# The first pair's queries and keys go ahead of the first weight block, and the planner's port rule is rewritten

## The chip, the cores and the metric

The kernel runs on one core of a Trainium2 chip. The metric is device time in microseconds of one execution; lower is better. Each time is the median of several runs.

## The reference

Two parts follow each other: attention with a threshold, and a gated MLP over its output. All arrays are float32 as seen by the caller; the batch is 8, with 8 heads of width 64 and 576 positions.

```python
scores = scale * q @ k.T                      # per batch and head, 576 x 576
thresh = max(scores, axis=-1) - tau           # tau = 0.02
scores = where(scores >= thresh, scores, -1e9)
attn = exp(scores - max); attn = attn / (sum(attn) + 1e-9)
x = attn @ v                                  # heads side by side: (8, 576, 512)
h = gelu_tanh(x @ w_in)                       # 512 -> 1024
u, v = halves of h
v_n = layer_norm(v) * g_ln
v_s = w_sg @ v_n + b_sg                       # over positions, 576 x 576
out = x + (u * v_s) @ w_out                   # 512 -> 512
```

The weights `w_in` and `w_out` reach the chip as 64-bit words; the kernel splits each into a high and a low float32 part itself.

## The kernel before

The work is written as 5368 *steps*, each a few instructions on one engine. Attention goes over 32 pairs of heads (4 pairs in each of 8 batch entries); a pair has nine score tiles of 128 rows. For a tile, TensorE forms scores (L807 for the first four pairs, L832 later), VectorE takes row maxima (L841), GpSimd subtracts the threshold (L847), ScalarE takes exponentials (L867), VectorE selects and sums (L874), TensorE transposes (L539), ScalarE copies the transposes out of PSUM (L982), and TensorE multiplies with the values (L1008). The MLP's products (L1105) of one batch entry are mixed in among the attention of the next.

The order in which steps are issued is fixed by a table, `PLACES` (L35): a compressed list with one position for each step. `order` (L319 on) sorts the steps by it; every engine then works through its own steps in that order, one after the other. The list holds steps of all engines, so moving a step in it changes something only if it passes another step of its own engine.

All loads are issued by SyncE (SP), in order, onto one queue. The first steps of each engine matter here:

- SP loads, in this order: weight block `w2` (L578; the block is 128 rows by 512 columns of `w_in`, 512 KB), the first pair's queries (L727, tile `rq`, 288.5 KB: they carry `tau` as an added column), its keys (L727, tile `rk`, 320 KB), the queries of a later pair, weight block `w0`, and so on.
- VectorE derives from `tau` the scale of the queries and the offset of the threshold (L555 to L557). Later it does three bit operations on the weight block (L596, L602, L604), then the first row maxima (L841).
- GpSimd converts the low words of the weight block in place (`w_bot`, L586), then scales the first queries (`q_scale`, L757), then clamps the weight block (`w_clamp`, L591), which VectorE's bit operations need.
- ScalarE takes absolute values of the block's upper words (`w_abs`, L582).
- TensorE does three short warm-up products (L545), the first scores (L807), then the products that give the low part of the weight block (L613).

While it is built, the kernel reckons with a clock of its own (`Planner.run`), from durations written into it. That reckoning does not set the order, which is the table's, but it chooses the PSUM banks: there are eight, and a tile of scores, transposes or products takes the bank (or the two) that the reckoning has free first (`place_in_banks`). In the reckoning, a VectorE operation flagged as using two SBUF ports and a GpSimd operation are not let run together. The flag is set in `_record` (L281 and L289): `ports > 1`, where `ports` counts the SBUF operands that are read, with one more for a `tensor_scalar` that reads SBUF.

Of the kernel before, what the change touches and what calls it, by code (L numbers as in the profile page):

```python
# [32 lines left out]


PLACES = (  # L35
    "c-qxi3v^Xgdd|1c>)w0r`;nU`c@q*KKnS4;s4&7PYqUN_eDtA?+Nzzk`cS)8+p(iEGuoLh3+S}EbjtF9k4~pJjujO}&~ZR!aOj9ZK^X%G0^t>d"
    "JjCSm`}es(kR&7lSM7y+&)NH&{Xf3{`~Us#<av4iKYl#@)wlB7Yc{X<?6K(+mL0wHexc{Ybv?Z#<;n2at#^F7*KA%tFZA_p_X!J*YV}SO)9<kF"
    "WqEzv^dozK;juffACWz$kUdzt`<CtD3}cel+wL59ynYe;g7<wr@8^lWcK43IH?WRAb$SEqIPOPYZ?^aOruPMz{RVnq9bR5uAA^3z1M4^uk`w$G"
    "0{+9+aS~^St78DH`qPoux6Z-%(L3jk>F@@xBX0;;<(<lp-WTswI=qweV<4<fl^=O07uP;>FsH*COg!?2ndkla(N{hUKF__O^XfF}Ro)Qe;hlaC"
    "eknS7Q_&m9V{fQ2?>8RDH;|#!_Po=J`Kj#o`ppk-==tHD*k1Lc(;GCe`ZBOz0YlEgywl{B*N4Yni5&C>s2!)J<BJ}9eN^nzsfmNhId6D-)NteB"  # L40
    "on~!6^D+0%u#Ub?0(<)2@B00m>iJ2{M*o|sH`H}Q9`$7zdiw1ezI4aWj62>?9Y6V;^MC8OH(>jAN=3u<-~0bS^)u?YH$2C_Y{$JplY7XH=W^Wp"
    "s!;vQi1^^websW@8+08TJX40{xHp_M@dkz3a9QmQ-ML<q@qN>mKmTXSQ)#4kr!P|TT6Sfk2pc_Thg+P_9Dt89u&3@T%pg$FJ`1;8c-4RWofRzY"
    "x)Fh@9-|?a+?zx?JR{z@HWB_bjCfOha__k&^7kgqom24&@SO>Gx&<GNcxc~u!m8rFId?PxhyeTNc~dN-3eiH`exuW4L;)A*xOn3PJ~zxHzL)Z<"
    "ldw5^Lvu^`(^iCmvma_l$+j98D5(3ZKmEhDF?ALYt-SjYu0gPT6IW(b?Q*CrD)wM^5D2B??*M_Q>#FrOVi=D%C@~Aic_V@l#$t0CTTM79!FzD6"
    "0vy4AJ4m6d7-$b6>mcl?>rq-f3$&$Ct>CL8u_3)93?q^?-=~Hee1=a9nqPzuU|Lxm#BagZCgQD8*snlo*rmL*LeTn|jWkL!Xnlp=j6f6xixIi&"
    "dqC1jV;$nQ8R~Mof-s$tpxtf>f_OVbB}wdng(Naq5#~)r@ZDN;C;}13F8!;p)WJ-Fw({8uI!G^r(^8#Fe@|q>;v6EQ)GlnJFej#V09KKuaKNB~"
    "Fn02{3<*39N}7g_B5;{uG?=TPj0$vPK>~$>F;Xt_QA}-j$HtjG#^<WzoUv`*)8|v4S)<kgrdi0Rv^^Rhi#NF<TZT>M;Q%Z%jqPIA6pET3Ae!gn"
    "#cQyL(Xnf>mN=>L1m|VK0u&{<;-)ndM)H1N{gib^4<4USn^hsUl9mq9Q#<+0tit*t2&e^kO@R3${6fsU0lTpbMo(lWUT(o^zHK+-4eAKR5x~bN"
    "=R4`dZ0b%w5h2NMDtze*PW^){wi3jHq7r<Q4uyD=Vj={Kh(jB!&qL?n1!9_*j;&Z_bHOaU&?;{lfia>AcAU}Q&Sjvl(`oJx?v+HUsqV-x-loD8"
    "9K;9;FK&QXb-+H7h+wnm2%uVhC=aILMJ|t3l8<YZQaBe&N8)2TU=^dCs`y?fDUlTWDh}HUyT6^Hj)u}U$*;@b;tw;bQz8~m?8g6)D#2#7(HP=u"  # L50
    "t8GHia<^SB<H?{`NKSkM&rik%1v@wjYk0vZ>?2m<M`fVL!1$$e#E*jdg*S8R*}M3YudtmEBoumL6vi8O7a10zq1ed>al`K9*e)S<8-f&B3>J*{"
    "Y&doXTltnzO2)k{DN;#yRrB=gT3e~({QUN_l^4C|UzpaR6di@KO0b8ZF>{j)42e`u_qIwgnTbUXrzT<}Hj`K8MR>Lm8zhorB@>~l@d-tg@OGqW"
    "*(kf?(u;Y2R>Oyt<kiCu&?)k1znC9UpHmBYrT-(5PbzfM%<ybHLmcc%$umhi>X?c(tXNhh){Bk_WZWiH@OHH7cBbPmW?skpu?;WIqK-v#gp?&X"
    "#21;uM}#e~Qv{cvCTcWjLnN+kV1`BUbLvcv!8@&3C6O$!b}OP%#=Ks|MCG&MgM@X-eXhi#`MdL|<H>tuKBytF(u7*#Vb{<svV;T{GlRI02?pCr"
    "k~UOop&A>r_$3{*%JIHpDJTvb<Uj$}hO&E7?(I`<E~Jh*A9dC9GWTK5XIw3sJU%E1t!!7q2W}J=-jzB$2EUQ?N|Haz1;=Lmx&^<ZRc1y!R%Q)K"
    "u~hq!sMt?_egD$g6h6CjYaRX2IcS&Rec{>&F5fQsGB&tW=oX<1AMqw0XGk@d51@_EglkhPn{~{Cfz(E-at(_5oG1`(+AtH}z545v*HU}?0$zS{"
    "w}4cF523kvNQW?1An|dE1FYww!@L|%QeJd2ZCGXz8W!{htjO_7(c4CT-z24hS_!OL@)X<y?zqSke@^8;epKu%HMUAkmU^`@hXpmECi`1-n+RFa"
    "$TrE;GUmsY7{!HfAR(lcdb}yd1@4H?$ZJN+%_I+@b@q%a%jm#$=8qmRyK&b-%8fZvuZ*PB)=h%x3@N_|W$1sKSbIGlls)w-bm29{m(IgW<E6kO"
    "G!82T#jzyGP89flFiA>LD{QNM^x8?Qam(v6SE;cglUyN`jJHYYiSzbjad4LNs;IWzxIhyQ*5Ta}$jVe&Clra;#W#tAO}x~f;JIrhzGtTw-pcE`"
    "3;2qYH9wTP8|1fx2&g1>nXp++vuI<*;6_Ul#f)0!&#zbk+|g(oi7m3S1RJH|R7ZMPOY(U)5e6q#e6xW%CRcA8&3HVxKn#qB)^V$rlBTgKZN?gM"  # L60
    "BpPKMq;lK66pLw3qK@^#kP?`+ww6dKPPkd?15U(Ki34<9VvaICx_0_wb<{Eaz~Pa+{PVrE*Db(CHaOub(up9UK=MU-sbX@qi{n5->KXEjNX?bB"
    "(rv-YR`Sa1b_&sMP-!i3Uco($xF$`$vHH4iQ25C7Cl$Qh_FohhC^Ln!Mw&7<a_mfI5-ZQD*I-jb3)TuSY-F%du{ch1mRzj48%v^HNRWXv9FiR6"
    "&Ouxdz5nVa3Xj&kehH@*%=I_GL(shi^tQ&BcSy|Z)owD2H&@{)hAHBhhop1_@yB?g06SFK-sC8(bd+aHMefvC71##F{O;Qb9Sk*9Zkfn<JTy->"
    "pIS?jHffOmd;Q|KS;ADu@dtz|I8F9i2NiLH4zaB(NBd-k2o6iw4pEwAyx-Qfy_P1c%PzZ7xO+wFwx@Wx_b~yZNK-Z;I+%lYewE}40!bXEvi#lY"
    "DorB0ka_r?LdYR^$BT}TienGcI#x*DZqPWC>qhgz*7+1ZHGji6@#A5MM=8x^2`?~r5j2in2EsnVGUiAv31G60N7P{Fx}5nDZo=wTsg8)1<2{3U"
    "E){yG?tR9PC+B0%U6LQ?R4%@TI+_oO-U2DNLD}=A&Supl^(M(tKt59$Nn0em3K|*8dX*b}q!1sE!8($b&7|~KsN)8+g;kkbk#oqj5)WT;4RzF3"
    "uWzD`pWQ)JBL;f7G~nQH_488X&&5i%ZWzs4zghNT=@kiGkXUvzaoiX>Gs1Gism0qYXpDx-+9Ek<mhKvnx@zX-qm@_JlK-vesN;wK%4xTTwVf1A"
    "P{#TMV!?Xdr$lTS3kQlcR^;b3Qh);_(AF#PI48`QL{ecK6XTaU<~6!0eSX3N!9(Zm7;(`rB<AyE>JQW^!R4%qE#~X~CcB#b5WYrRk5C1-pm#-5"
    "Iq`Y`dVhcMLVw4cgkQ;m39MF>bcI&%Sp+lS?>7QoRNoiU)BE*ZFfG3^T3jP-jQ^OqmBrtRV@YmDqC*Zi#X?<_i*3O$gLz9#P7Z7#Egn|zq+;xB"
    "oP{tGGu|#3fHfmvv7W3m<=DipK~AB&UR1=d)S3c6k%k}m8((o_SYJZ^s8a*QiYT8S-L0zwinNWH`4u5iJI!C<@0D&!Iv->^^h~;2$MWX2)ndB="  # L70
    "-_a7>CXFx8M)I5BI)Nt^NEZ2hj?Ml^I!|9}ifyonE`sAvB#Fg8lJj4KQGjB>W|<Tk8$a-$Kd#S$)PoqW%Vhz|C+ZCfPsp?hX@yv8KafWbrk2Vh"
    "Iez%|=}(P+WckRq`ZCmilO>|UfA(wrLbTk{qnw?&xM}y%aGqfQ>P>&GM-lxyno8$t({#r}M@{CGeM~?pUA$8ogV<3+s$o%TJfSymjTrtdXv=wJ"
    "qAz5zKB#d-VwA~9MCI$%b^j@&8<;FnslCr=Wx7goBBwE^4NGRw%gR)dKWNj{%APN;UCGK96W<e-VUqV<{5l3QCwS}+tSQiEnyUrA5`Qj@D*Tgy"
    "W1o6DR_gCBRlZjt+#_;a|9M#Rv5^z@QD|MvRY>qWSC-I7FO#@AJg-q~B=e|%F+$e?g!5krY3a>ACtnU3etSvl)4Ib+N|`H_KMmw;3M6y%6;Ces"
    "sWy9j6HhjT@3}IO#N!6FhSW2ST$NC{Q2XJ}|DnD#pXEn2*6UH6j?VS7J_m%uZb_=J58Wh^|5lxA5l1Sl{Ar=g(G3MpEcz7}3s}RLX3b&62!$4k"
    "k&U>(7x)?!dDi%jR#^L-w3#St(T^rSCi)%ha3fL&KJ}Ayyk&@qIg?gt;#YV1hl2IoW;E5S6c2N6>DT3N0`gfQ0S*y^s5<7&oe$~?<9=O7aor+)"
    "uJZA%WCZRMC~^poq9K#~Nap)cr}$jDG@ptwa??s4Cm|<dc!b!pt_dG2T`U$ZIQUE0Q9k=IlGag}3mfm3-3{jy>B5MAXS5@JJ{qzs>RmSr*F^Ma"
    "2}wr{-x{rM6XXvCm?5BEB4r@XlWE-VgisjNnS$P_K1%<7>(-lfuKZN*sXix0QsNz%<5eU}P?~g(`i@o6@!KWffl$B~SP0W$0yu#nRF3_RW^{I!"
    "M@490i6)u4-WRw?MC%6Bpvd2dUN!xQPcCWDCI$SX&Ba&(|Ic6kx@G?5r9_T+y1MP7egg4x%@^#^{FROgEWr7>DC-3`+~@CEm-ussG#m|oU*iKK"
    "zLt`R_vZ37mScj?V7)8r{;&6FihoglE=Bd`nRA~(3SxDBuH@;h9zpw!;$v*mX`#W|Yv%S+9IL8et&)9RtwmuNmRjS7Vmn-kz&1bGe=kixee<KV"  # L80
# [1312 lines left out]
```

## Time and profile before

| | us |
|---|---|
| median of 3 runs | 970.79 (970.67 to 971.47) |
| profiled execution | 967.75 |
| its span, first to last instruction | 966.0 |
| TensorE busy | 946.5 (98%) |
| VectorE busy | 662.7 (69%) |
| ScalarE busy | 664.3 (69%) |
| GpSimd busy | 562.8 (58%) |

The busy times are of the one profiled execution and add over the whole span; the engines work side by side. The mean granted TensorE clock of that execution was 0.996 of full speed. A line such as L757 is a line of the kernel's file; tiles go by their names without buffer numbers, so `rq` is a tile of raw queries, `rk` of raw keys, `w` a raw weight block, `room` its working copy, `nm` a tile's row maxima, and `all_banks` is PSUM.

### The profile page before, as it was taken

Reading aid. Unit: us, or ns where it says so; the run is one execution under the profiler, and the core shown is the slowest. Engines: PE = TensorE matmul, PEld = TensorE weight load, DVE = VectorE, ACT = ScalarE, POOL = GpSimd, SP = SyncE. Lnnn points to the kernel's source line nnn. Section 1 sums busy time; section 2 is a strip of 40 time slices with the busy share of each in tenths; the row PEclk is TensorE's granted clock in tenths of the full one; section 3 lists DMA queues with packets and bytes.
Section 4 is the critical chain, followed back from the end, with each engine's and each line's share of the span. In section 5 each row is a group of like instructions: output and inputs, shape, how many; then the busy total and the mean of one; then the engine's idle time right before and its main releaser. Section 6 shows DMA issues by size and latency. Waiting matters only on the chain.

```text
span 966.0 us, 19828 instructions
## 1 busy us (share of the span) xinstructions
PE 946.5 (98%) x6822; PEld 811.0 (84%) x6822; DVE 662.7 (69%) x1409; ACT 664.3 (69%) x1395; POOL 562.8 (58%) x997
## 2 busy tenths in 40 slices
...
GB/s 291 138 121 111 20 112 71 124 128 137 113 97 107 123 127 91 86 114 124 91 108 98 135 124 92 90 110 139 117 80 102 99 142 122 93 65 38 14 13 50
DMA packets 60236, 100.39 MB, mean 104 GB/s; under 512 B 15220, under 2 KB 23655, under 8 KB 60136
## 3 DMA queue, kind: packets, MB, share of 16 engines
...
## 4 chain that ended last, share of the span: by engine, by line
PE 83%; DVE 6%; ACT 5%; POOL 3%; issue 2%; DMA 2%; SPq 0%; POOLq 0%; ACTq 0%; DVEq 0%
PE all_banks L1105 38%; PE all_banks L1008 15%; PE all_banks L832 14%; PE all_banks L539 13%; DVE nm L841 1%; ACT p L867 1%; PE all_banks L807 1%; DVE p L874 1%; DMA qz<-qhi 1%; PE all_banks L613 1%; ACT pt L982 1%; POOL ot L1308 1%; DVE vv L1088 1%; PE all_banks L991 1%; DMA rq<-in_qT 1%
## 5 line engine op out<-in xcount | busy, mean ns | idle before, releaser
L841 DVE TENSOR_REDUCE nm<-all_banks 128x1 f32<-128x576 f32 x288 | 209.9, 752 | 59.4 <-PE all_banks L832 52.4
L867 ACT ACTIVATE p<-all_banks,nm 128x576 f32<-128x576 f32 x256 | 185.0, 740 | 88.0 <-DVE nm L841 86.4
L874 DVE SCALAR_TENSOR_TENSOR p<-all_banks,nm,p 128x576 f32<-128x576 f32 x256 | 204.0, 814 | 56.0 <-ACT p L867 28.3
L982 ACT ACTIVATE pt<-all_banks 128x512 f32<-128x512 f32 (+1 forms) x320 | 164.6, 554 | 23.1 <-PE all_banks L539 22.5
L539 PE MATMUL all_banks<-ident_r,p 128*128 128x128 f32 x1152 | 172.0, 275 | 2.8 <-ACT pt L982 1.4
L832 PE MATMUL all_banks<-ks,qst 128*128 128x288 f32 x560 | 157.2, 314 | 0.3
L539 PEld LDWEIGHTS all_banks<-ident_r,p 128*128 128x128 f32 x1152 | 135.9, 141 | 21.0 <-issue 4.1
L1008 PE MATMUL all_banks<-pt,rv 128*64 128x320 f32 (+1 forms) x1024 | 138.1, 411 | 0.1
L847 POOL TENSOR_TENSOR nm<-columns,nm 128x1 f32<-128x1 f32 x288 | 53.9, 192 | 143.7 <-DVE nm L841 132.2
L832 PE MATMUL all_banks<-kl,qz 128*128 128x288 f32 x448 | 123.6, 295 | 0.0
L1105 PE MATMUL all_banks<-wsh,z 128*128 128x288 f32 (+2 forms) x512 | 113.1, 299 | 1.4 <-ACT z L1206 0.9
L832 PEld LDWEIGHTS all_banks<-ks,qst 128*128 128x128 f32 x560 | 102.4, 189 | 11.9 <-issue 6.3
L1008 PEld LDWEIGHTS all_banks<-pt,rv 128*64 128x64 f32 x1024 | 69.6, 136 | 49.2 <-issue 7.0
L1105 PEld LDWEIGHTS all_banks<-wsh,z 128*128 128x128 f32 x512 | 85.0, 188 | 2.4 <-ACT z L1206 1.1
L832 PEld LDWEIGHTS all_banks<-kl,qz 128*128 128x128 f32 x448 | 84.7, 189 | 0.3
L1105 PE MATMUL all_banks<-xh,wih 128*128 128x288 f32 (+2 forms) x256 | 78.3, 306 | 0.0
L1105 PE MATMUL all_banks<-gh,woh 128*128 128x288 f32 (+2 forms) x256 | 76.2, 301 | 0.0
L1105 PE MATMUL all_banks<-gh,wol 128*128 128x288 f32 (+2 forms) x256 | 76.2, 299 | 0.0
L1105 PE MATMUL all_banks<-xh,wil 128*128 128x288 f32 (+2 forms) x256 | 76.2, 298 | 0.0
L1105 PE MATMUL all_banks<-xl,wih 128*128 128x288 f32 (+2 forms) x256 | 76.0, 297 | 0.0
L1105 PE MATMUL all_banks<-wsl,z 128*128 128x288 f32 (+2 forms) x256 | 75.3, 296 | 0.0
L1105 PE MATMUL all_banks<-gl,woh 128*128 128x288 f32 (+2 forms) x256 | 75.2, 295 | 0.0
...
## 6 DMA issues: line engine op xcount, KB each, us to landing
...
```

What stands on the lines that cost most here:

```text
L539: nc.tensor.transpose(out, x, ident_r.bitcast(F32))
L613: nc.tensor.matmul(t["acc"], a, x, start=(j == 0), stop=(j == 2))
L807: nc.tensor.matmul(st["s", h, i][:, a, 0:HALF], st["q"][rows, qo:qo + P], st["k"][rows, lo:lo + HALF], start=True, stop=True)
L832: nc.tensor.matmul(sc[:, a, 0:HALF], w, x, start=(j == 0), stop=(j == len(terms) - 1))
L841: nc.vector.tensor_reduce(nmax, st["s", h, i][:, :, 0:HALF], AX.XY, ALU.max, negate=True)
L847: nc.gpsimd.tensor_tensor(thr, toff, st["nm", h, i], ALU.subtract)
L867: nc.scalar.activation(target(h, i), st["s", h, i][:, :, 0:HALF], AF.Exp, bias=st["nm", h, i])
L874: nc.vector.scalar_tensor_tensor(dst, st["s", h, i][:, :, 0:HALF], st["thr", h, i], dst, ALU.is_ge, ALU.mult, accum_out=st["l"][:, c:c + 1])
L982: nc.scalar.activation(dst, src, AF.Copy)
L991: nc.tensor.matmul(tp[:, 0:D], pm[:, MAIN:KW], both, start=True, stop=True)
L1008: nc.tensor.matmul(acc[h * D:(h + 1) * D, 0:w], st["v"][:, o:o + D], unit(h, a)[:, kt, 0:w] if kt < NM else tail_unit(a)[:, 0:w], start=(k ...
L1105: nc.tensor.matmul(st["acc"], *term(j), start=(j == 0), stop=(j == n - 1))
```

## The change

Two edits. The first replaces the table of positions. Read out, the lists agree in everything but their first 18 entries, and there in the place of five steps: the loads of the first pair's queries and keys, the first step on `tau`, and two of the warm-up products.

```
place   before                      after
0       warm-up product             load queries, first pair
1       warm-up product             load keys, first pair
2       load weights w2             load weights w2
3       w_bot w2        (GpSimd)    tau 1           (VectorE)
4       load queries, first pair    w_bot w2        (GpSimd)
5       tau 1           (VectorE)   tau 2           (VectorE)
6       tau 2           (VectorE)   tau 3           (VectorE)
7       tau 3           (VectorE)   warm-up product
8       q_scale         (GpSimd)    q_scale         (GpSimd)
9       w_abs w2        (ScalarE)   warm-up product
10      w_clamp w2      (GpSimd)    w_abs w2        (ScalarE)
11      w_word w2       (VectorE)   w_clamp w2      (GpSimd)
12      w_word w2       (VectorE)   w_word w2       (VectorE)
13      w_hi w2         (ScalarE)   w_word w2       (VectorE)
14      w_word w2       (VectorE)   w_hi w2         (ScalarE)
15      w_mul w2        (GpSimd)    w_word w2       (VectorE)
16      warm-up product             w_mul w2        (GpSimd)
17      load keys, first pair       warm-up product
18      first scores    (TensorE)   first scores    (TensorE)
```

Taken engine by engine, only SP's order differs: before it loads `w2`, queries, keys; after it loads queries, keys, `w2`. The orders on TensorE, VectorE, ScalarE and GpSimd are the same in both lists.

The second edit is the flag: a VectorE operation now counts as using two ports only if it is a `tensor_scalar` with all its operands in SBUF and more than 64 elements in each of 128 rows. It emits no instruction; it enters the reckoning that chooses PSUM banks.

```diff
 PLACES = (
-    "c-qxi3v^Xgdd|1c>)w0r`;nU`c@q*KKnS4;s4&7PYqUN_eDtA?+Nzzk`cS)8+p(iEGuoLh3+S}EbjtF9k4~pJjujO}&~ZR!aOj9ZK^X%G0^t>d"
+    "c-qxi3zSvWdA{F1uY2#g@5kJEGVd8?cnz<iGoV6*C@WeY5g$#eMs3w*tv=MQ)iyRNX|zd}1vITLwXCT4XqsS*6%|F)7?1=*BMu5m96%5lo`O8Y"
...
         first = writes[0] if writes else reads[0]
-        ports = sum(not a.psum for a in reads) + (op == "tensor_scalar" and not reads[0].psum)
+        ports = 2 * (op == "tensor_scalar" and not any(a.psum for a in (*reads, *writes)) and reads[0].size > 64 * P)
         rows = first.shape[0]
```

More of the change, by code (lines that the diff above doesn't have):

```diff
@@ L35 @@
 PLACES = (
-    "c-qxi3v^Xgdd|1c>)w0r`;nU`c@q*KKnS4;s4&7PYqUN_eDtA?+Nzzk`cS)8+p(iEGuoLh3+S}EbjtF9k4~pJjujO}&~ZR!aOj9ZK^X%G0^t>d"
[L37 to L80, printed above, removed]
@@ L81 @@
-    "|7iWy+O{8+(z~iF-=k0TR{g(Fl?OT"
+    "c-qxi3zSvWdA{F1uY2#g@5kJEGVd8?cnz<iGoV6*C@WeY5g$#eMs3w*tv=MQ)iyRNX|zd}1vITLwXCT4XqsS*6%|F)7?1=*BMu5m96%5lo`O8Y"
+    "nbYsz=Q0d3Gt3OQVlUi#&fe$j|MC6b|L=cKzzg{Q`0?~t-^y=~*+9?P?&;%}9li8?q3if{T|FcPWY~S{9h>ek8|dSO-rnsD^f10#t9QJZK8L+8"
+    "3-of+hwOfa-FIFeBD+o^d!TmrF5AOt#w5_w?mTzAJ`wwz_q{#u<B7g@_Kd&Rzm8sYdj0D-=0~6>+k1V}`<%=^1Kqz4FA(Tu(8suc9mhj*oF9Y0"
+    "f5<vc;LK2U^n+DjIs(1x9Ecx1bFN#5H*g(+L0}a)nIAnb-pO=$C*((eSe-0C0w)&NUUM+7!y8CE0z=I6zWnGd9|oT1-r#w43iT>5$ar|Co`YYA"
@@ new lines @@
+    "j-FKX`t#TuY|Q(N$FU7$Ftt5!YB4{V-Cm#h;SD}NyyM%eK6H8m=2dS7_9<Y{IT$!aUU|KE{H4f2ub<j+N;*F8vDZt*K9!m{keu^|wnq&$9^NU|"
+    "_R}A8?=<V^?If_P_x-NV&&i&j&}{U*nR<g=H|SAsmZ7W9uHg%J{Peiv4c74!&pCfw$Gv{rx05Ows{h{q2dbY|$GxFB_C-7H4Vc`6c08Zs-j{{y"
+    "Uqr+QzV6GG<KBSl*ua@GB*(p>q=`2m)P~AxZ}86bm`omMedFhUp*)pAW@qLCHMeC)Hin4Nb!Ma`_^AWvNA{FGMOg$Z+h^jY^RM`?f3QMj`>sc@"
+    "y2}_HPwh@26PcdayE+;9B!a|*#?<b!O%&`-ncJt}CEz<_@nj1=9QMGT??hDPJ+p6{03ZtNpX*JwjB3P+aO?F>mk|S8pyR^zWBJ@LQ}|xmt4YD;"
+    ">~+m8kxyC?0nU7&9i>}pVW6<#Z~pvG+eS86K&<M{hYSUExM>4dW>x(wP&riY!p;y7&LrLjf-%=sYi-2Qgx4uC2gi9miZDiDV+NZ|I4H%taIHcd"
@@ new lines @@
+    "!T&f&qr3!Y4<qLw;;3s;Rx%T`Wt>{ZSL?7Yvn>K6nls;{hFW}zj}4k%jQ3$$IUL0Az}Lp(&EeRuKxx>ayo^G~`k9RkO0#HviQWuD426pjz2kd8"
+    "%E@3261ExM=k5!^bm~C6-BN_`R+vgs*aizJWU(y5o668T_2^IpB7q(HS7C{R83Jw9)0K3PUWTTo_b&MZ;f#oLhz?gfu!X{$xY`C-#g@VWg9;+p"
+    "&fjt*@gyi|Dmse6Wri`@TmfZNq7(CzD1v;_E(%aWZFk1Um|ezas^hFtZQhgTQlD9?)&Qni#HX}9mKcRMxFT1M4d&q>EHi_xV%B7eninLR=i>RR"
+    "u#nNQ>#>?RsV0K+B4GiFlU#Abs<Cyv-_tmGjnRci=h0?Wgw3R-L-f>kJ~OMawip6xAzl?={tUkqGq1x=EQQe(oq-oyu##`v&3K(U!U+WN5i0mj"
+    "COM0`Gmk|{@*9d?xQtW(B#W&i@t~+A-=srf-lUlbp<?3D2J5r%S$K|^CZ}ODR@huH6VJ8En?`V?sDhnf^tW;u=<76^`~ABmk!ou?3QD%9NF@hx"
@@ new lines @@
+    "g2Ia%Bvu`;k0hhmC^~|uQ6I>Isd%2t<5lG2YNZs;#*#XGL<g)Av{Mz|+e=EM#J<YIw!+SDr>SFfS)1h7rEl_w8MRj;mPqcz|B@=9X0*{5;%lod"
+    "LeL7gT`o;z&`TsIzJ_NfVV!~<8je-GU^w;=EAgW$*kzz;$!zhXuyMhSoO=2W{uC%|B?L)@t~iD9#@#`NMQJFu^FhL}_i}8P61#OFiYx&O#=ABg"
+    "JB!VH%P1q`-jWolqPwbj+BL1M)NyV>`<cp%-SuxkD4eFFP*y2+5j19Qih&`KD(K#3DJC<p(Bag0tj9+3%DezikHb2N<S5BRs2Y4s5v9DXGc6nC"
+    "w_SW8@6Q<hK^1xR;C*z8eA+MON7ZN4LSE_rNEVO^due857M>ywc9rCrq#bok!75fPs|ssH$5=9M11fntLUlUR@K-ag;r*!5&(EZeg|mf}r8vYF"
+    "nZieeEwIxBm!ApLXwZgeLfgO$i{Tg4nHq_=Td_hSS!nH4M5Ua0y@H9#XC(&->*9M{iAVEy=TgVxcgcK6Lt?RL3r%3x(k!xs1Qs(xIG+gy+e(o("
@@ new lines @@
+    "RBE9H>vQ-O9keR&o?<B|i5TQSA=id;yVCBhlW#1dj@cjXYvg6lgPhO0S~PilP!d|%u7nRNOL6b;CNvVimGnxHKd%Um&G=0Veow2+taz-<T9jdl"
+    "_9I!jpZxlli)T^ztg_7w^h4*MU5@vJYs0vFtK`e5&=R3rlrDV8n?!;k)m%P+HbN7rPcLuQF%JdP>#52$DC#q!K)7kc41D*>uTox1{jKwPdFW07"
+    "sT3bTbMuf6VZ2b{<CFwh&qarMDITZ1*d*Gp)FL!2=%cYL&nrc5$MO3HDGk(1VAbL$;2v<tL?8Q0D*y4rVrQALS!%M>tMz#-s0p>X-=Wh)*osBB"
+    "NT!xEKQ_fFE{p?7A+6No4RJ1ThkZ(3Gg@vobqKAqre9u82d*)H_!F}ecPyaXxFhw-NJ(woAec^<@{4em{<n#>*W!NJQ?I~2ysG%pIe4K-3OvGN"
+    "uv}0aMUresq3;Kiqzv`Kw)%&!p12Y>y(V*28Y?o%6++2)i<F)OZ$A<TXF4y7YTHc+G?7pP-YJEwOlNdLk%;^FCULNdm-;52xmx0TW@f?7yskNq"
@@ new lines @@
+    "uQ)mL1F5?qemjVON@0fyo7FUjHdYL7v?Nj7sAvBCniaqufwnqql9i=cFBPXI+QnK@z`OBaM}TEtA59&TYPO7EJno+_1}4I5xK&F@)7X?XV--0P"
+    "i?I$;x$RzzMYJc`z<Oaw3CvlWOQjSi-JJD4Clcx80lF?RM>!u|J?)VO>X>%ma2+o{x|{a8g;>u9CsIv15hN5!z9=tULay%PIGB`rhJs>Jb2+Va"
+    "Td=&9yfQnTBD5P+T2GvpaZe+zDU)xkyyj~ZUYGf}l9yY4PGP}vQz&a>C}Tax&Lk$W@~lP;Hbt~xwE)9L1`8C6<5Xwyg_^tZ6xxLZSxCbn$x-1P"
+    "#CfrMube>Pv4+<!;?(>({swpmy0?Jd))?~+iFu>iNoMip3OvCuMIG~yl#UR-fyWB5O_lFX4aagvdA3yKy&9`R+n|`=e;eV0;R#in#xoud%$3cj"
+    "-jbwE8RY+NzxZvGFg0-eKA{RtmA%$MWx}9CZ0jn}K8YcM!xFYll;#-kw{&f<r^)J)ORg90UY5S)3104gM8GK4lue2b=Ad0rE%}0A3WuqzU}vUU"
@@ new lines @@
+    "lgKV&9=@v(cF5f((GgY&>|$ESi^$t`8VBhc5W2s09)(XSST{!ecu?X|Msr!h3(Xw_jboRAu#d2eIZ{i4n55$oGuXMl!u*I#z{*ysj)+&_U4wZp"
+    "6?(hweMXWe=VJC9k{@SPExL+2nh%NILMgW)+4H5&=F~*>2FX!KK2sS<TP(Z^8ClADnHzny2p^5a8j_aHr1V#4;0CjaRhe6nbI7!k4_<T?b=23a"
+    "oj@HwyN#$u4Rmp7(81xFXQjxWjpc0JFoLyyqwK}fD-ya8vFv2xxN+>w3d;?r9&fRrF&Zvwi{zkLwqscOiW!%VP+mhz!MC2FjvxFxr`=lCc2YD+"
+    "8Ecb>hZ=RC618P494OXUk)Kyd0S=Ntn=iwooG{}ONrf>?j9=-P*XpM9*|GP94xO`Y*ag3on9r4|KT#_Lmoq9inXmbq>`L}S_zG=3LKWPC-VsR^"
+    "#Oprj{r&m#{T*{6ek}{evRYBnWm>_fQA~%w-w1dyeP2XR@6~sqjQqxFajmp5{$u7=4u3C>rMMl54mseI2z5~*wuK@L=1p-qIk1Jacv!*Xim|hC"
```

12 lines of the change are left out of this document (added).

## The prediction

> **What bounds the kernel now.** I read the page's totals first, then the chain of waits at the start, then the queues that feed that chain. The totals, from the page:
>
> ```profile
> span 966.0 us, 19828 instructions
> ...
> PE 946.5 (98%) x6822; PEld 811.0 (84%) x6822; DVE 662.7 (69%) x1409; ACT 664.3 (69%) x1395; POOL 562.8 (58%) x997
> ```
>
> TensorE (PE) is busy for 946.5 of 966.0 us, in a fixed order. So once its stream runs, whatever delays the start of the stream delays the end by as much, and only its 19.5 us of idle time could give anything back. The change is at the start. The chain of waits there, in order of time (start us, us, what):
>
> ```profile
> 1.18 4.89 DMA rq<-in_qT
> ...
> 6.09 0.15 DVE columns L555
> 6.24 0.07 DVE columns L556
> ...
> 6.34 0.82 POOL rq L757
> ...
> 7.24 0.62 POOL room L591
> ...
> 7.89 0.71 DVE all_banks L596
> ...
> 8.62 0.70 DVE room L602
> ...
> 9.41 0.43 DVE w L604
> 9.84 0.68 DVE nm L841
> ```
>
> The first queries land at 6.07 us (1.18 + 4.89), the scale is derived from them (L555, L556), GpSimd (POOL) scales them (L757). But the chain does not go on to the first scores. It goes through the first weight block: its clamp on POOL (L591), its three bit operations on VectorE (DVE, L596, L602, L604), and only then the first row maxima (L841), which stand behind those in DVE's queue. Each step starts within 0.1 us of the end of the one before it, so this stretch has no slack to give.
>
> **The change, part by part.** It is a matter of queues. SyncE (SP) issues the transfers; POOL takes its work in order. Both timelines (start us, us, engine, line, operation, count, and in brackets the idle time before), and what SP waited for in the first 12 us:
>
> ```profile
> 0.73 0.39 SPq L578 DMA_DIRECT2D w<-in_w_in  x1
> 1.18 0.42 SPq L727 DMA_DIRECT2D rq<-in_qT  x1
> 1.64 0.43 SPq L727 DMA_DIRECT2D rk<-in_kT  x1
> ...
> 5.31 0.40 SPq L727 DMA_DIRECT2D rk<-in_kT  x1
> 6.08 0.33 SPq L660 DMA_DIRECT2D w<-in_w_sgT  x1
> 7.19 0.33 SPq L578 DMA_DIRECT2D w<-in_w_in  x1
> 7.92 0.33 SPq L727 DMA_DIRECT2D rk<-in_kT  x1
> ```
> ```profile
> SPq L578 <- DMA rk<-in_kT: 0.8, 1, 0.8
> ...
> SPq L660 <- DMA rq<-in_qT: 0.4, 1, 0.4
> ...
> SPq L727 <- DMA w<-in_w_in: 0.3, 1, 0.3
> ```
> ```profile
> 5.37 0.65 POOL L586 TENSOR_SCALAR w<-w 128x512 f32<-128x512 uint32 x1 [4.07 <-DMA w<-in_w_in]
> 6.34 0.82 POOL L757 TENSOR_SCALAR rq<-rq,columns 128x576 f32<-128x576 f32 x1 [0.32 <-DVE columns L556]
> 7.24 0.61 POOL L591 TENSOR_SCALAR room<-room 128x512 f32<-128x512 f32 x1
> ...
> 11.54 0.74 POOL L757 TENSOR_SCALAR rq<-rq,columns 128x576 f32<-128x576 f32 x1
> 12.36 0.66 POOL L586 TENSOR_SCALAR w<-w 128x512 f32<-128x512 uint32 x1
> ```
>
> From its ninth transfer on SP issues each one when an early one lands, so its restarts are landing times: the weights at 5.31 (the ninth waits for the first), the queries at 6.08, the keys at 7.19, a later pair's queries, fourth in the queue, at 7.92.
>
> (1) *The moved transfers.* The queries are now issued at 0.73, the keys at 1.18, the weights at 1.64. The three together are the same bytes as before, so the last of them, now the weights, should land when the last of them did before, the keys at 7.19: 1.88 us later than the weights' 5.31. The bounds: with nothing ahead slowing it, the weights need the 4.58 us of before (5.31 - 0.73) from their new issue, and land at 6.22; if the fourth transfer's packets mix with theirs, they land with it, at 7.92. I take 7.19, because the four landings come one after the other, which says queue and not parallel service. The queries land at 5.31 or sooner (first place, fewer bytes than the weights that landed then), the keys by 6.08 at the latest, the second place's landing of before. The transfers behind these three keep issue and landing within the bound just given.
>
> (2) *What the early queries release: nothing.* DVE derives the scale at once, so the 0.32 us that POOL idled ahead of L757 goes. But the order of POOL's queue is untouched: L586, which reads the raw weights, stands ahead of L757. The wait for the weights, 4.07 us at 5.37, grows, and the scaling of queries that have long been there is stuck behind it; then L591 behind that. From the weights' landing: 0.06 to POOL's start (5.31 to 5.37), L586 0.65, a gap of 0.08 (11.54 + 0.74 to 12.36), L757 0.74 (the undisturbed later row; the 0.82 ran beside a DVE operation that now runs earlier), a gap of 0.08. L591 starts 1.61 us after the landing: at 8.80 instead of 7.24, **1.56 us later**. By the bounds: 7.83 (0.59 later) and 9.53 (2.29 later).
>
> (3) *TensorE and ScalarE at the start.* The first scores follow L757's end, 8.72, instead of 7.16. They must be done when DVE gets to the first maxima, at 9.84 + 1.56 = 11.40. Rows for the warm-up products, for these scores and for later sets, and the granted clock in stretches of 2 us (the column PEclk, 1.00 is full):
>
> ```profile
> 1.61 2.93 PE L545 MATMUL all_banks<-pm 128*128 128x256 f32 x6 [1.61 <-DVE pm L520]
> 7.31 1.24 PE L807 MATMUL all_banks<-rk,rq 64*128 64x288 f32 x8 [2.77 <-DMA rk<-in_kT]
> ...
> 12.28 2.29 PE L807 MATMUL all_banks<-rk,rq 64*128 64x288 f32 x8
> ...
> 17.50 1.33 PE L807 MATMUL all_banks<-rk,rq 64*128 64x288 f32 x8 [0.98 <-ACT tt L997]
> ```
> ```profile
> 6.00:8.00 2.00, 0.69 (x6) 0.68 (x8) 1.35 (x7) 0.00 (x0) 1.45 (x3) 1.00 1.04 408
> 8.00:10.00 2.00, 1.19 (x7) 0.59 (x4) 1.86 (x4) 0.63 (x1) 0.01 (x1) 0.63 1.04 408
> ...
> 14.00:16.00 2.00, 2.00 (x14) 1.50 (x11) 1.97 (x4) 0.76 (x2) 2.00 (x3) 0.67 1.03 416
> 16.00:18.00 2.00, 1.02 (x7) 0.62 (x8) 1.79 (x4) 2.00 (x5) 0.98 (x3) 1.00 0.97 392
> ```
>
> The clock falls to half between 8 and 10 us. The scores would now run in that stretch and cost 2.29 us, not 1.24: from 8.87 to 11.16, just before 11.40, so nothing is added; if they took 0.5 us longer, 0.3 would be added. ScalarE's part of the weight block starts when they land and is done before L591. The two warm-up products and the scale's first step also change place in the written list, but on no engine's own order: cost nothing.
>
> (4) *The rule for shared ports* in the planner adds no instruction. The planner's clock decides which of the eight PSUM banks a tile gets (the first free in its reckoning), and both the rule and the later weights move that reckoning. So the bank of a tile can differ from early on, through the whole kernel. The trace of before cannot show the new map. What it shows is the idle time of TensorE behind readers of a bank, from 25 to 930 us (total, times, longest):
>
> ```profile
> PE all_banks L539 <- ACT pt L982: 1.4, 2, 1.1
> ...
> PE all_banks L807 <- ACT pt L982: 1.0, 1, 1.0
> PE all_banks L991 <- ACT wil L625: 0.9, 1, 0.9
> ...
> PE all_banks L539 <- DVE uu L1088: 0.5, 1, 0.5
> PE all_banks L1105 <- DVE ir L1017: 0.4, 1, 0.4
> ```
>
> These are 4.2 us in 6 waits, 0.7 us each. A new map can gain at most these 4.2; for the other side I take as many again, +4.2. My value is 0, midway: the same greedy choice is made by a clock that differs little.
>
> The sum: +1.56 + 0 + 0. The profiled execution took 967.75 us (span 966.0 and 1.75 around it), so its like would be 969.31. The median of the runs, 970.79, lies 3.04 above it; I forecast against the median: 970.79 + 1.56 = **972.35 us**.
>
> **The rivals.**
>
> *Hidden after all (970.8).* The weights' chain is late, but the pipeline behind it catches up. For it: VectorE and ScalarE are each busy only 69% of the whole. Against it: the chain is unbroken from 6 us, and no transfer stands on it after the queries', so nothing that keeps its old time is waited for later.
>
> *The clock stays half for longer (973.7).* TensorE now idles from its warm-up's end at 4.54 us (1.61 + 2.93) to 8.87 instead of to 7.31. If full clock returns after 19 us instead of near 15.5, the scores on the chain at 17.50 take twice 1.33: +1.33 more, 970.79 + 1.56 + 1.33 = 973.68. Against it: in the changed kernel the weight products and second scores keep TensorE busy from 11 to 16 us, as in the stretch of before after which the clock rose. The Trainium skill (TensorE: Matmul & The Clock Gate, Part 1) states that the gate watches a free-running window of about 3.4 us and that the count of slow products varies from run to run; by that rule the phase, not this change alone, picks this case. The clock rows agree as far as a low stretch of some 7 us goes, and show no phase.
>
> *The bank map costs (975 to 977).* Place: the transposes (L539), whose bank must have been copied out by ScalarE (L982). Price 0.7 us a wait; six more give 970.79 + 1.56 + 4.2 = 976.55. From the first such wait on (+2.26) the change is beyond what counts as none. For it: the order was fixed together with the old map. Against it: TensorE waits so seldom now that the banks have room.
>
> *The bank map gains (other side, 968.2).* Place: the same 4.2 us of waits, most of them singles of about 1 us. If all went: 970.79 + 1.56 - 4.2 = 968.15. It decides the sign once more than 1.56 goes, and is faster beyond doubt only from 3.5. For it: the old reckoning kept GpSimd from running beside a select on DVE (a score tile in PSUM, a threshold column and one SBUF tile), and in the chip's rows the scaling at 11.54 beside a select took the usual 0.74, so the new reckoning fits better. The Trainium skill (SBUF — State Buffer, Who interferes with whom) says that VectorE contends with GpSimd in two-port modes or with two SBUF inputs; the 0.74 agrees with it for a select that reads one SBUF tile.
>
> *It does not do what it says* is part of my forecast: the queries come first, yet nothing starts sooner.
>
> **How the numbers follow.** Forecast 0.57; hidden 0.08; clock 0.10; bank costs 0.12; bank gains 0.13. A difference under 0.2% (1.94 us; 968.85 to 972.73) cannot be told from none. The forecast's own range by its landing bounds is 971.38 to 973.08, and with a bank wait more or less 970.7 to 973.8; about a third of it, 0.20, lies beyond 972.73. Slower: 0.20 + 0.10 + 0.12 = 0.42. Same: 0.37 + 0.08 = 0.45. Faster: 0.13. The range reaches down into the gains to 969.0 and up into the costs to 975.5; outside are some 0.10 below and 0.08 above.
>
> **What would show it.** Right: SP's eleventh issue still at about 7.2 us; POOL's L586 starting there after some 6 us idle, L757 at about 8.0, L591 at 8.8, the first L841 near 11.3; TensorE's busy time unchanged. Step 1 is wrong if L586 starts outside 6.3 to 8.0; step 2 if L757 runs ahead of L586 or the maxima ahead of L604; step 3 if the first maxima wait for scores; step 4 if idle time of TensorE behind readers of a bank between 25 and 930 us differs from 4.2 by over 1 us. The prediction falls if the start moves by 1.5 us and the end does not.

## The result and the profile after

The change made the kernel slower: 976.17 us (median of 10 runs, 973.07 to 977.97) against 970.44 us of the kernel before in the same series (968.98 to 971.60), a ratio of 1.0054 with a 95% interval of 1.0042 to 1.0067. That is 5 to 6 us, where 1.56 were forecast, and the time lies above the range that was given. The profiled execution took 976.15 us. Five of the executions behind this document, of 1166 to 3526 us, were in a slow state and are left out of every median and ratio. From the page of the profiled execution:

```profile
span 974.4 us, 19822 instructions
...
PE 949.4 (97%) x6822; PEld 812.3 (83%) x6822; DVE 662.6 (68%) x1409; ACT 665.4 (68%) x1395; POOL 564.4 (58%) x997
```

Beside the page of before, 8.4 us have come to the span, of which TensorE's busy time took 2.9 (949.4 - 946.5); its idle time grew by the other 5.5 (25.0 - 19.5).

SyncE's own queue after the change (start us, us, line, what is issued):

```profile
0.73 0.39 SPq L727 DMA_DIRECT2D rq<-in_qT  x1
1.17 0.42 SPq L727 DMA_DIRECT2D rk<-in_kT  x1
1.64 0.43 SPq L578 DMA_DIRECT2D w<-in_w_in  x1
...
6.05 0.57 SPq L660 DMA_DIRECT2D w<-in_w_sgT  x1
7.81 0.33 SPq L578 DMA_DIRECT2D w<-in_w_in  x1
8.56 0.33 SPq L727 DMA_DIRECT2D rk<-in_kT  x1
```

The three transfers stand in their new order. The eleventh issue, which waits for the third transfer (now the weights), has gone from 7.19 to 7.81, and the twelfth, which waits for the fourth, from 7.92 to 8.56. GpSimd's timeline in the same stretch, with the idle time before an instruction in brackets:

```profile
7.87 0.65 POOL L586 TENSOR_SCALAR w<-w 128x512 f32<-128x512 uint32 x1 [6.57 <-DMA w<-in_w_in]
8.61 0.75 POOL L757 TENSOR_SCALAR rq<-rq,columns 128x576 f32<-128x576 f32 x1
9.44 0.61 POOL L591 TENSOR_SCALAR room<-room 128x512 f32<-128x512 f32 x1
```

The order of this queue is the old one, and everything in it is late: the clamp L591 by 2.20 us (9.44 - 7.24). VectorE's timeline shows both ends, the scale derived at once and the rest behind the clamp; the last line, for comparison, is from the kernel before:

```profile
4.40 0.15 DVE L555 TENSOR_SCALAR columns<-rq 128x1 f32<-128x1 f32 x1
...
10.09 0.69 DVE L596 TENSOR_SCALAR all_banks<-room 128x512 uint32<-128x512 uint32 x1 [4.87 <-POOL room L591]
...
11.95 1.42 DVE L841 TENSOR_REDUCE nm<-all_banks 128x1 f32<-128x576 f32 x2
```
```profile
9.75 1.42 DVE L841 TENSOR_REDUCE nm<-all_banks 128x1 f32<-128x576 f32 x2
```

The queries are there by 4.40, and the first row maxima start at 11.95, 2.20 later than before (9.75). TensorE, from its timeline:

```profile
9.41 2.29 PE L807 MATMUL all_banks<-rk,rq 64*128 64x288 f32 x8 [4.87 <-POOL rq L757]
...
14.48 1.24 PE L807 MATMUL all_banks<-rk,rq 64*128 64x288 f32 x8 [0.69 <-DVE p L874]
...
78.55 1.23 PE L539 MATMUL all_banks<-ident_r,p 128*128 128x128 f32 x9
80.87 0.54 PE L539 MATMUL all_banks<-ident_r,ir 128*128 128x128 f32 x2 [1.09 <-ACT pt L982]
```

The first scores cost 2.29 us instead of 1.24 and end at 11.70, before the maxima. So the start accounts for some 2.2 us. Set against the trace of before, instruction by instruction, TensorE's lag (how much later the same instruction starts) jumps at three more places, each of which has its view.

*At 20 us, the clock.* Windows, here of one microsecond but for the first (length, then PE, PEld, DVE, ACT and POOL busy, then the granted clock, the share of the DMA engines and GB/s), and then TensorE's timeline:

```profile
9.00:11.00 2.00, 1.59 (x6) 1.19 (x8) 0.88 (x2) 0.00 (x0) 0.97 (x2) 1.00 1.04 409
...
19.00:20.00 1.00, 0.29 (x2) 0.30 (x4) 1.00 (x3) 1.00 (x3) 0.19 (x2) 0.81 0.02 7
20.00:21.00 1.00, 1.00 (x6) 0.91 (x7) 0.83 (x3) 0.63 (x2) 0.33 (x2) 0.50 0.00 0
21.00:22.00 1.00, 1.00 (x6) 0.26 (x2) 0.00 (x0) 0.00 (x0) 1.00 (x1) 0.50 0.00 0
22.00:23.00 1.00, 1.00 (x5) 0.52 (x6) 0.91 (x3) 0.11 (x1) 0.09 (x2) 0.50 0.00 0
23.00:24.00 1.00, 1.00 (x9) 0.53 (x6) 0.84 (x2) 1.00 (x2) 0.92 (x3) 0.98 0.76 225
```
```profile
19.70 2.38 PE L807 MATMUL all_banks<-rk,rq 64*128 64x288 f32 x8 [1.51 <-ACT tt L997]
```

A mean of 0.81 means that 0.38 of that microsecond went at half clock, and 0.98 means 0.04: half clock from 19.62 to 23.04, 3.42 us. The third pair's scores fall into it and take 2.38 us instead of 1.33; up to the end of the stretch the lag grows from 2.21 to 3.74, by 1.53.

*At 81 us, a bank.* The last row of TensorE's fence above has no idle time before it in the trace of before. There, from the TensorE and ScalarE timelines:

```profile
75.55 0.38 PE L539 MATMUL all_banks<-ident_r,ir 128*128 128x128 f32 x2
```
```profile
74.88 1.65 ACT L982 ACTIVATE pt<-all_banks 128x256 f32<-128x256 f32 x4
```

The `ir` transposes ran while ScalarE was still copying the third pair's transposes out of PSUM (74.88 to 76.53). After the change ScalarE's copies are these:

```profile
79.16 1.65 ACT L982 ACTIVATE pt<-all_banks 128x256 f32<-128x256 f32 x4
```

They end at 80.81 and the `ir` transposes start at 80.87, behind the last of them. In the planner's map, the last of these sets of the third pair's transposes (the tile `t2_0_3`) has moved from bank 3 to bank 4, and the `ir` transposes use banks 4 and 5 in both maps. In all, 123 of the 1097 PSUM tiles have another bank. The lag rises by 1.26 at this place.

*From 81 to 84.5 us, the clock again,* behind that wait:

```profile
79.00:81.00 2.00, 0.91 (x8) 0.66 (x7) 1.93 (x6) 1.98 (x8) 1.88 (x3) 1.00 0.41 98
81.00:83.00 2.00, 2.00 (x10) 1.08 (x12) 1.82 (x7) 1.05 (x3) 1.86 (x4) 0.52 0.80 177
83.00:85.00 2.00, 2.00 (x14) 1.04 (x10) 0.59 (x2) 0.42 (x1) 0.72 (x1) 0.63 0.60 180
```

The lag grows by another 1.7, to 7.0. Of the eight profiles with the new map of banks, here and below, this one alone has this second fall. What is left of the 8.4 comes in steps of 0.3 to 0.6 from 230 us on.

### The profile page after: what moved, and what is told of

It is laid out like the page before. It is cut to its first block, busy times and chain, and to the rows that moved or that the text cites. A ratio compares the mean times of both kernels' runs of the same rounds, so it can differ in the third digit from the quotient of the medians.

```text
span 974.4 us, 19822 instructions
## 1 busy us (share of the span) xinstructions
PE 949.4 (97%) x6822; PEld 812.3 (83%) x6822; DVE 662.6 (68%) x1409; ACT 665.4 (68%) x1395; POOL 564.4 (58%) x997
## 4 chain that ended last, share of the span: by engine, by line
PE 83%; DVE 5%; ACT 4%; POOL 3%; issue 3%; DMA 1%; SPq 0%; POOLq 0%; ACTq 0%; DVEq 0%
PE all_banks L1105 38%; PE all_banks L1008 16%; PE all_banks L832 14%; PE all_banks L539 13%; DVE nm L841 1%; PE all_banks L807 1%; DMA qz<-qhi 1%; ACT p L867 1%; DVE p L874 1%; PE all_banks L613 1%; ACT pt L982 1%; POOL ot L1308 1%; POOL vv L1200 1%; PE all_banks L991 1%; DVE vv L1088 0%
```

## The experiments

None of the kernels leaves out work. Some add warm-up products whose results are not used. Differences in us are between medians; each ratio is to runs of the kernel before on the same chip.

### One half at a time

**loads_alone** is the kernel before with the three loads in the new order and the PSUM banks of before:

```diff
...
+        first = [step("q_load", "a0"), step("k_load", "a0"), step("w_load", "w2")]
+        order[:] = first + [i for i in order if i not in first]
```

> The kernel before with the queries, the keys and the weights as the first three transfers, and nothing else: the PSUM banks stay those of before. Theory A (three causes: the late weights cost 2.2 us, the bank map about 1.2, and each adds to the idle time after which the clock of TensorE falls to half): 972.5 to 974.5, L586 at 7.8 us, and the inverse's transposes (L539 on ir, near 78 us) wait no longer than in the kernel before. Theory B (the load order is all of it, the banks cost nothing): 975.5 to 977, as the whole change. Theory C (the banks are all of it, the late weights are caught up): 970 to 971.5.

Measured: 973.11 against 971.17, +1.94, ratio 1.0020 (1.0010 to 1.0029). Its GpSimd and TensorE timelines:

```profile
9.21 0.65 POOL L586 TENSOR_SCALAR w<-w 128x512 f32<-128x512 uint32 x1 [7.91 <-DMA w<-in_w_in]
```
```profile
78.77 0.38 PE L539 MATMUL all_banks<-ident_r,ir 128*128 128x128 f32 x2
```

With the old banks the `ir` transposes do not wait. The weights landed later still than in the profile after, at 9.14 and not near 7.8 as expected.

**rule_alone** is the kernel before with the new flag only:

```diff
-        ports = sum(not a.psum for a in reads) + (op == "tensor_scalar" and not reads[0].psum)
+        ports = 2 * (op == "tensor_scalar" and not any(a.psum for a in (*reads, *writes)) and reads[0].size > 64 * P)
```

> The kernel before with the new port rule alone: the transfers as before, the PSUM banks those of the changed kernel. Theory A: 971.5 to 973.5, start as before (L591 at 7.2 us), and the inverse's transposes near 75.5 us wait about 1.1 us for a bank that ScalarE's copies (L982) still read. Theory B: 970 to 971. Theory C: 975 to 977.

Measured: 972.53 against 971.17, +1.36, ratio 1.0014 (1.0002 to 1.0025). Its bank map is that of the kernel after. TensorE's timeline:

```profile
17.34 2.38 PE L807 MATMUL all_banks<-rk,rq 64*128 64x288 f32 x8 [1.51 <-ACT tt L997]
...
77.70 0.44 PE L539 MATMUL all_banks<-ident_r,ir 128*128 128x128 f32 x2 [0.98 <-ACT pt L982]
```

The wait at the `ir` transposes is there with the loads in their old order. It stood, at 0.77 to 1.09 us, in every profile taken with the new map, here and below, and in none with the old one. So this wait belongs to the flag and not to the loads, and half clock at the third scores (2.38 us here) needs no late start.

**after_again** is the kernel after once more, and **fill** is the same with two more warm-up products at the one that runs near 17.6 us, to shorten the idle time before the third scores:

```diff
-            nc.tensor.matmul(x[:, 0:2 * P], pm[:, 0:P], pm[:, 0:2 * P], start=True, stop=True)
+            for _ in range(3 if k == 2 and bank_of(f"warm{k}") != BANKED else 1): nc.tensor.matmul(x[:, 0:2 * P], pm[:, 0:P], pm[:, 0:2 * P], start=True, stop=True)
```

> The changed kernel once more, on the chip of the other three and with another profile. Theory A says that the half-clock stretches fall elsewhere or are missing: a run without them within 1 us of 973.2, one with both near 976 to 978, the first L591 at 9.4 us in each. A theory without the clock: the same stretches, and 976.2 within 0.5.

> The changed kernel with two more warm-up products on TensorE beside the one near 17.6 us, in time that TensorE idles; banks and transfers as in the changed kernel. Theory A with the clock as a cause: no stretch at half clock between 16 and 25 us, the third scores (L807, x8) take 1.3 us and not 2.4, time 1 to 2 us under the changed kernel's in the same call. If the clock is no cause of the loss: within 0.5 us of it, or up to 1.2 us above, should the products delay the scores.

Measured: after_again 976.18, +5.01, ratio 1.0047 (1.0033 to 1.0061); fill 975.04, +3.87, ratio 1.0039 (1.0026 to 1.0052). In fill's timeline the third scores run at full clock:

```profile
20.37 1.33 PE L807 MATMUL all_banks<-rk,rq 64*128 64x288 f32 x8 [0.64 <-ACT tt L997]
```

The medians say that the fall near 20 us is worth about 1.1 us, but the two intervals overlap. The two halves by themselves cost 1.94 and 1.36, 3.30 in all, and the whole 5.01: more than the sum.

### The queues at the start

**scale_first** is the kernel after with GpSimd's L757 ahead of L586, **clamp_first** the kernel before with GpSimd's order L591, L757, L586. In the edits `low`, `scale` and `clamp` are the steps of L586, L757 and L591:

```diff
...
+        order.remove(low)
+        order.insert(order.index(scale) + 1, low)
```
```diff
...
+        order.remove(low)
+        order.remove(scale)
+        at = order.index(clamp) + 1
+        order[at:at] = [scale, low]
```

> The changed kernel with one step moved on GpSimd: the scaling of the first queries (L757) goes ahead of the conversion of the weights' low words (L586). If the queue order on GpSimd is what keeps the early queries from helping: L757 starts at about 4.6 us, the first scores before 7, and the clamp (L591) 0.8 us after the weights' landing and not 1.6, so everything behind it 0.8 us sooner, 975.3 where the changed kernel has 976.2. If the late weights alone set the start, with no part for the queue: L757 early all the same, but the time unchanged within 0.3.

> The kernel before, its transfers and banks untouched, with GpSimd's first three steps on data in another order: clamp of the weights (L591), scaling of the queries (L757), conversion of the low words (L586). If the chain from the weights through the clamp to the first maxima sets the start: L591 at about 6.0 us instead of 7.24, the first maxima about 1.1 us sooner, and the time about 1 us under the kernel before. If the queries' landing sets it (6.07 us in both): no gain, within 0.3 us of the kernel before.

Measured: scale_first 973.40 against 969.85, +3.55, ratio 1.0034 (1.0022 to 1.0047). GpSimd's timeline:

```profile
4.66 0.82 POOL L757 TENSOR_SCALAR rq<-rq,columns 128x576 f32<-128x576 f32 x1 [3.36 <-DVE columns L556]
8.17 0.65 POOL L586 TENSOR_SCALAR w<-w 128x512 f32<-128x512 uint32 x1 [2.69 <-DMA w<-in_w_in]
8.90 0.61 POOL L591 TENSOR_SCALAR room<-room 128x512 f32<-128x512 f32 x1
```

Once it is free of L586, the scaling runs as soon as the queries are there, and the clamp starts 0.79 us after the landing (8.90 - 8.11) instead of 1.63. So the order of this queue does hold up the early queries, as forecast; but the early queries still buy nothing, because the clamp has to wait for the weights, and the kernel stays slower than before. Against the 5.0 to 5.8 that the kernel after costs in its own series, 3.55 is a gain of 1.5 to 2.2, more than the 0.8 by which the clamp moved; the kernel after was not in this series, and what the rest is was not tested.

Clamp_first came to 969.63, ratio 0.9997 (0.9987 to 1.0006): no difference, although the clamp starts 1.24 us sooner. GpSimd, TensorE and VectorE:

```profile
6.00 0.61 POOL L591 TENSOR_SCALAR room<-room 128x512 f32<-128x512 f32 x1 [4.71 <-ACT room L582]
```
```profile
7.62 2.29 PE L807 MATMUL all_banks<-rk,rq 64*128 64x288 f32 x8 [3.08 <-POOL rq L757]
```
```profile
9.94 1.42 DVE L841 TENSOR_REDUCE nm<-all_banks 128x1 f32<-128x576 f32 x2 [1.05 <-PE all_banks L807]
```

The first scores ran at half clock, and the maxima waited 1.05 us for them. That is step 3's cover, gone: where the weight block is early, the cold scores are what the start waits for.

### How much of it is the profiled execution

**before_again** is the kernel before, profiled a second time; **fill_before** adds the two warm-up products of fill to it.

> The kernel before once more, for a second profile. If the first profiled execution was a lucky one (its 967.75 us lie 3 us under the median): this one takes 970 to 972, and against the first one the later steps on TensorE come in at most a few jumps, a fall of the clock to half of some 1.5 us among them or waits for transfers of about 1 us. If it was typical: 967.5 to 968.5 and no jump over 0.5 us.

> The kernel before with the two more warm-up products beside the one near 16 us. If its median, some 3 us above its one profiled execution, holds a fall of the clock to half early on in most runs: 1 to 2 us under the kernel before, and no half-clock stretch between 15 and 22 us. If the clock has no part in that difference: within 0.5 us of the kernel before, or up to 0.9 above, as the products take the time of TensorE.

Measured: before_again took 971.20 us, where the first profile took 967.75; the runs lie at 969.85. TensorE's timeline and a window:

```profile
17.67 2.09 PE L807 MATMUL all_banks<-rk,rq 64*128 64x288 f32 x8 [1.51 <-ACT tt L997]
```
```profile
19.00:21.00 2.00, 2.00 (x10) 0.76 (x8) 1.32 (x3) 0.53 (x1) 1.46 (x3) 0.50 0.03 6
```

The kernel before has the fall near 20 us too, in some executions: it cost 1.63 us of lag here, and the profile from which the forecast was made happened not to have it. The rest of the 3.45 us between the two profiles comes later, 0.8 near 288 us and 0.7 near 835 us among it. Fill_before: 969.38 against 969.85, ratio 0.9993 (0.9984 to 1.0001), no difference that can be told. So falls near 20 us can explain little of the 3 us by which the median of the kernel before lies above its first profile.

### The landing of the weights

**loads_again** and **after_third** repeat loads_alone and the kernel after; **queries_first** is the kernel before with the loads in the order queries, `w2`, keys:

```diff
...
+        first = [step("q_load", "a0"), step("w_load", "w2"), step("k_load", "a0")]
+        order[:] = first + [i for i in order if i not in first]
```

> The kernel before with the three transfers in the new order, as in the first run of it, banks of before; beside the changed kernel in the same call. If the two edits add up: 2 us above the kernel before, and the changed kernel some 1.4 us above this one. If the bank map costs more where the start is late: the changed kernel 2.5 us or more above this one.

> The changed kernel a third time, beside the order of the loads alone. If the edits add up: 3.4 us above the kernel before. If they do more together: 4.5 to 5.7, as in its two comparisons so far. In its profile the inverse's transposes after 75 us wait 1.1 us again, whatever the clock does.

> The kernel before with queries, weights, keys as the first transfers: one transfer ahead of the weights and not two. If each transfer ahead delays the weights by its own length: they land about 0.8 us later than before, at 6.1, L591 at 7.7, the time 0.4 to 0.8 us above the kernel before. If being third among several is what makes the weights late (7.8 to 9.1 us where the keys in third place landed at 7.2): they land by 6.4 and the time is that of the kernel before within 0.5.

Measured: loads_again 973.27 against 970.25, +3.02, ratio 1.0030 (1.0018 to 1.0042); after_third 976.03, +5.78, ratio 1.0060 (1.0047 to 1.0073); queries_first 970.70, ratio 1.0007 (0.9998 to 1.0015). After_third's GpSimd and TensorE:

```profile
6.89 0.65 POOL L586 TENSOR_SCALAR w<-w 128x512 f32<-128x512 uint32 x1 [5.60 <-DMA w<-in_w_in]
```
```profile
18.71 1.33 PE L807 MATMUL all_banks<-rk,rq 64*128 64x288 f32 x8 [1.51 <-ACT tt L997]
...
78.60 0.44 PE L539 MATMUL all_banks<-ident_r,ir 128*128 128x128 f32 x2 [0.99 <-ACT pt L982]
```

This execution had an early landing (6.83) and no fall near 20 us; it took 974.03 us, the shortest of its six runs, and the wait at the `ir` transposes is there all the same. In queries_first the weights land at 5.94, so one place back costs some 0.6 us of landing, and the time cannot be told from before. Its third transfer, here the keys, landed at 8.18. In the eight profiles with the old order the third landing stood at 6.75 to 7.19. That points to the queries in first place, and not to the weights being third; it is one profile, and why is open.

### The clock cared for, and the sum of the halves

**warm_and_clamp** is clamp_first with three more warm-up products before the first scores and two more near 16 us. **warm_before**, **warm_loads**, **warm_rule** and **warm_whole** put the same products into the kernel before, into loads_alone, into rule_alone and into the kernel after:

```diff
...
+            for _ in range({2: 3, 0: 4}.get(k, 1) if bank_of(f"warm{k}") != BANKED else 1): nc.tensor.matmul(x[:, 0:2 * P], pm[:, 0:P], pm[:, 0:2 * P], start=True, stop=True)
```

> The kernel before with the clamp first on GpSimd, three more warm-up products ahead of the first scores and two more near 16 us. In clamp_first the first scores ran at half clock (2.3 us) and the first maxima waited for them. If that is what ate its gain: here the scores take 1.2 us, the first maxima start at 8.9 instead of 9.8, and with the clock kept up later the time is 1 to 2 us under the kernel before. If the start does not set the end: no better than fill_before, 0.5 us under it.

Measured: 967.81 against 970.25, ratio 0.9973 (0.9961 to 0.9984). It is faster than both kernels. TensorE's and VectorE's timelines:

```profile
7.71 1.24 PE L807 MATMUL all_banks<-rk,rq 64*128 64x288 f32 x8 [0.89 <-POOL rq L757]
...
16.61 1.33 PE L807 MATMUL all_banks<-rk,rq 64*128 64x288 f32 x8 [0.65 <-ACT tt L997]
```
```profile
8.97 1.42 DVE L841 TENSOR_REDUCE nm<-all_banks 128x1 f32<-128x576 f32 x2
```

With full clock the first scores are done by 8.95, and the maxima, 0.97 us sooner than in clamp_first, wait for nothing.

> The kernel before with three more warm-up products ahead of the first scores and two more near 16 us, so that the clock of TensorE does not fall early: the base of this call, 968.5 to 969.5, with little scatter.

> The same products, with the order of the loads alone (banks of before). The late weights by themselves: 1.6 to 2.3 us above the base with these products. If the fall of the clock was part of what the order alone cost: under 1.5.

> The same products, with the port rule alone (banks of the changed kernel). The wait at the inverse's transposes near 76 us and smaller ones: 1.2 to 2 us above the base.

> The same products, with both edits. If what the two edits did beyond their sum was the clock falling more often in the first 25 us: the two distances above add up here, 3 to 4 us above the base. If the gap stays without early falls of the clock: 5 us or more above it, and then the clock is not its cause.

| | us | ratio to the kernel before | over warm_before |
|---|---|---|---|
| kernel before | 970.22 | | |
| warm_before | 969.25 | 0.9983 (0.9974 to 0.9992) | |
| warm_loads | 970.82 | 1.0008 (0.9999 to 1.0017) | +1.57 |
| warm_rule | 970.26 | 1.0007 (0.9998 to 1.0016) | +1.01 |
| warm_whole | 972.77 | 1.0031 (1.0020 to 1.0041) | +3.52 |

With these products the whole costs 3.5 instead of 5.0 to 5.8, so 1.5 to 2.3 us of the loss go once TensorE's idle stretches at the start are shorter. The halves cost 2.58 together, 0.94 less than the whole; before it was 1.7 less. Each of these differences is uncertain by about 1 us, so whether the halves only add up is not settled. Two profiles bear on it. GpSimd in warm_loads, then TensorE in warm_whole:

```profile
6.63 0.66 POOL L586 TENSOR_SCALAR w<-w 128x512 f32<-128x512 uint32 x1 [5.34 <-DMA w<-in_w_in]
```
```profile
10.01 2.24 PE L807 MATMUL all_banks<-rk,rq 64*128 64x288 f32 x8 [3.05 <-POOL rq L757]
...
79.85 0.44 PE L539 MATMUL all_banks<-ident_r,ir 128*128 128x128 f32 x2 [1.09 <-ACT pt L982]
```

The products did not hold the clock up to the late first scores of warm_whole (2.24 us), and the weights landed at 6.57 in the one and at 8.40 in the other. So the landings of single executions differ by more than the gap.

## Why the prediction was wrong, and where it was right

**What bounds the start: right.** The chain through the weight block is the one that counts. Nothing starts sooner for the early queries, and the end follows the start.

**Step 2, the queue of GpSimd: right.** L757 stands behind L586, and L591 starts 1.63 us after the landing (9.44 - 7.81), as against 1.61 forecast. Scale_first shows that the order of the queue is the cause of half of that.

**Step 1, the landing: right in kind, too small.** The weights were to land where the last of the three had landed, at 7.19, with 7.92 as the latest. In nine profiles with the new order they landed between 6.57 and 9.14, the middle one at 7.86, near the upper bound; four of the nine were later than that bound, loads_alone by 1.22 us. The same bytes did not take the same time. In the profile after, the third and the fourth landing are both 0.6 us later than before, so the landings still come one after the other, but later. Among the transfer records, single packets of 4096 bytes, which usually take 0.16 us, took up to 0.52 us in the profile before, 0.54 in the profile after, and 1.13 to 1.61 in the four with the latest landings. So a few slow packets go with the latest landings, but they do not set the profile after apart from the one before. Why is open; no run tells it. The term of 1.56 should have been about 2.2, with 1.0 to 3.5 by execution. The test that was set for this step (L586 between 6.3 and 8.0) was met by the profile after, at 7.87, and was too wide to find this.

**Step 3, the cold first scores: right.** They cost 2.29 us, as forecast, and end 0.25 before the maxima want them. Clamp_first shows the other side of that cover.

**Step 4, the bank map at nothing: wrong.** The value 0, "midway", is the step that failed most clearly: the planner's new reckoning moves 123 tiles to other banks. The flag alone costs 1.36, or 1.01 with the clock cared for, and in the profile there is one new wait of 1.09 us with a lag of 1.26. The test that was set could not have decided it. TensorE's waits between 25 and 932 us after the change (total, times, longest):

```profile
PE all_banks L539 <- ACT pt L982: 2.7, 4, 1.1
...
PE all_banks L807 <- ACT pt L982: 1.0, 1, 1.0
...
PE all_banks L539 <- DVE uu L1088: 0.9, 1, 0.9
...
PE all_banks L1105 <- DVE ir L1017: 0.3, 1, 0.3
```

These rows sum to 4.9, against the 4.2 taken from the trace of before, within the 1 us that was allowed. The first row has gone from 1.4 in 2 waits to 2.7 in 4, though (2.5 in 4 in rule_alone, still 1.4 in 2 in loads_alone), and that is the place that the rival *the bank map costs* named. It was given 0.12, at six new waits and 976.55 us; the time came out near that figure, but one new wait does not make it.

**The clock: given too little.** The rival *the clock stays half for longer* had 0.10 and a price of 1.33 on the third scores. The price was about right (1.53 and 1.54 in two profiles of the kernel after), the mechanism only in part. It is not one long low stretch: in the profile after the clock is full at the second scores and falls again near 20 us, for 3.4 us. Such a fall stands in two of three profiles of the kernel after, in one of two of the kernel before, and in rule_alone, clamp_first and loads_again. The Trainium skill (TensorE: Matmul & The Clock Gate, Part 1), cited there, has a free-running window of 3413 ns; the stretch of 3.42 us agrees, and so does that the same kernel falls in one execution and not in the next. The sum of the forecast had no term for such a fall, and the profile that it was read from had none that costs anything. How much it is in the times can be read from the mean granted clock of each execution: of the 22 of the kernel after, three have 1.000 and took 973.26, 973.34 and 974.03 us, and the 19 others have a median of 976.32. In the kernel before the same split gives 970.20 (36 executions) and 970.63 (66). So without falls the kernel after lies some 3.1 us above the kernel before, close to the 3.30 of the two halves, and the falls add up to 3 more, where the warm-up products gave 1.5 to 2.3. With three such executions that is an indication and not a proof.

**The sum.** Against 970.44: some 2.2 for the start, 1.0 to 1.4 for the banks, and 1.5 to 2.3 by which the extra products make the whole cheaper, together 4.7 to 5.9, where 5.2 (by the ratio) to 5.7 (by the medians) were measured. That is an estimate from parts, each uncertain by about 1 us; the split between the start and the clock is the least sure. Of the 4.2 us that the forecast fell short by the medians, the clock is the largest part, the banks come next, and the late landing is the smallest, some 0.6.
